# Converting fp64 weights: the mantissa's scale moved into VectorE's last product, the sign moved onto the power of two

## The chip, the cores and the metric

The kernel runs on one core of a Trainium2 chip. The metric is the device time of one execution in microseconds, lower is better. One program on one core is measured; three runs of the kernel before took 819.85, 822.35 and 826.33 us (median 822.35).

## What is computed

Two blocks follow each other. The first is a recurrence over 768 time steps for 4 batches x 8 heads with a 40 x 40 state; the second is a two-matrix feed-forward block over the 3072 tokens which the first produces, with `h * cos(h)` between the matrices.

```python
# recurrence, per batch and head: state is 40 x 40
y[:, :, t] = einsum('bhd,bhde->bhe', r_t, state)
Sa = einsum('bhde,bhe->bhd', state, a_t)
state = state * w_t[:, :, None, :] - outer(Sa, b_t) + outer(v_t, k_t)
# feed-forward: x is y as (3072, 320)
h = x @ w_in                 # 320 x 2048
g = h * np.cos(h)
out = (g @ w_out).astype(np.float32)   # 2048 x 320
```

The inputs of the recurrence are float32. The weights `w_in` and `w_out` reach the kernel as float64, because their scaling by `1/np.sqrt(...)` widens them. The chip's engines have no float64 arithmetic in this kernel, so each weight is put together from the two 32-bit words of its float64. `w_in` is also multiplied by 1/(2 pi), so that `h` comes out in turns, and `w_out` by 2 pi, which takes that back.

## The kernel before

**Two interleaved streams.** The recurrence is computed in 24 chunks of 32 time steps. Each chunk `c` has a chain of five segments, `t`, `q`, `x`, `s`, `z` (functions `ch_t` to `ch_z`): TensorE makes products in PSUM, ScalarE and VectorE copy or mask them to SBUF, the next segment's matmuls read those. The last segment, `ch_z`, updates the state `qz`: VectorE adds (line 656), GpSimd multiplies by the decay (line 657, four instructions), then GpSimd multiplies the outputs `yt` (line 668). The next chunk starts by transposing `qz` on TensorE (`ch_t`, line 558) and copying the result on ScalarE (`s`, line 562). The feed-forward block is cut into pieces (`first_a`, `first_b`, `second`) that are placed between the segments (`M` in the lists of segments), and fills TensorE for most of the run.

**The order is written out by hand.** The loop at line 920 lists the segments of each chunk; `step(work, of_inv, of_w)` runs one segment, then whatever was put off until then, then up to `of_w` steps from the list `w_steps`. Each engine takes its instructions in this order, so an instruction that waits holds up everything behind it on its engine.

**The weights' conversion** is 20 items of 128 x 512 numbers. Function `rounded` returns four closures for an item: `fetch` (SyncE issues the DMAs of the raw words), `taken`, `mantissa` and `product`. In what follows T(n), STT(n) and P(n) are VectorE's instructions of item n in those three:

- T(n), lines 241 and 242: from the high word, the 20 mantissa bits, and the 11 exponent bits. ScalarE then makes the power of two from the exponent (`expo`, line 245) and the sign as +1 or -1 (`sign`, line 247).
- STT(n), line 251: adds the low word times 2^-32 to the mantissa bits. ScalarE then makes `1 + m/2^20`, already times the factor, in one pass (`mant`, line 254, called ident(n) below).
- P(n), line 257: mantissa times power, written to the weights' tile. GpSimd then multiplies that tile by the sign in place (line 260).

The list `w_steps` (lines 840 to 849) puts them in the order P(n), fetch, STT(n+1), T(n+2), P(n+1) and so on; so T(n) stands two groups ahead of P(n). The tiles `mant`, `expo` and `sign` have two buffers each. GpSimd has other work in the same queue: the copies `vp`, `rp` (line 490), which wait for the DMAs of `v` and `r`, and `kn`, `vvm` (lines 497, 498). SyncE issues all loads of the recurrence and the weights in one queue.

**TensorE's fillers.** `busy` (line 856) puts matmuls on an unused tile between the first segments, whose results nobody reads.

Of the kernel before, what the change touches and what calls it, by code (L numbers as in the profile page):

```python
# [9 lines left out]
F32 = mybir.dt.float32  # L10
I32 = mybir.dt.int32
U32 = mybir.dt.uint32
ALU = mybir.AluOpType
ACTF = mybir.ActivationFunctionType
# [6 lines left out]
def kernel(  # L21
# [43 lines left out]
    nc = tc.nc  # L65
    B, H, S, D = r.shape
    P, C, DP = 128, 32, 64
# [22 lines left out]
    def kept(name, shape, n=1, fill=None, part=lambda t: t, on=nc.gpsimd):  # L90

        tiles = []
        for i in range(n):
            t = const.tile(shape, F32, tag=f"{name}{i}", name=f"{name}{i}")
            if fill is not None:
                on.memset(part(t), fill)
            tiles.append(t)
        return tiles
# [8 lines left out]
    src = {"r": r, "k": k, "v": v, "w": w, "a": a, "b": b}  # L107
# [12 lines left out]
    for n, fill in (("w", 1.0), ("a", 0.0), ("b", 0.0)):  # L120
        for i in range(4):
            x = slice((i - 2) * H * DP, (i - 1) * H * DP)
            if i < 2:
                t = const.tile([P, H, DP], F32, tag=f"nat_{n}{i}", name=f"nat_{n}{i}")
            else:
                t = {
                    "w": w_in_sb[:, 0, late:], "a": w_in_sb[:, 1, late:], "b": late_out
                }[n][:, x].rearrange("p (h d) -> p h d", h=H)
# [4 lines left out]
    for n in "kvr":  # L133
        t = const.tile([P, H, D], F32, tag=f"nat_{n}", name=f"nat_{n}")
# [69 lines left out]
    bn_b = kept("bn", [P, H, DP], 7, 0.0, padding)  # L204
    kn_b = kept("kn", [P, H, DP], 2, 0.0, padding)

    by_in = kept("by_in", [P, 1], 1, 0.5 / math.pi)[0]
    by_out = kept("by_out", [P, 1], 1, 2.0 * math.pi)[0]
    to_bits = kept("to_bits", [P, 1], 1, (127.0 - 1023) * 2**23)[0]


# [5 lines left out]
    WID = 512  # L217
    first_done, second_done = [], []

    def rounded(m, dst, src, by, by_sb):  # L220

        pool, tag = (
            ((sb2, "gT"), (sb2, "gT"), (sb1, "nt"), (sb1, "u"), (sb1, "inv"))[m % 5]
            if m < 10 else ((sb1, "nt"), (sb1, "u"), (sb1, "inv"))[(m - 10) % 3]
        )
        t = {}

        def fetch():  # L230
            t["words"] = pool.tile([P, WID, 2], I32, tag=tag, name="words")
            for rows, cols, part in src:
                nc.sync.dma_start(
                    t["words"][rows, cols].rearrange("p n w -> p (n w)"), part.bitcast(I32)
                )

        def taken():
            hi = t["words"][:, :, 1]
            t["mant"] = sb2.tile([P, WID], I32, tag="mant", name="mant")
            t["expo"] = sb2.tile([P, WID], I32, tag="expo", name="expo")  # L240
            nc.vector.tensor_scalar(t["mant"], hi, 0xFFFFF, None, ALU.bitwise_and)
            nc.vector.tensor_scalar(
                t["expo"], hi, 20, 0x7FF, ALU.logical_shift_right, ALU.bitwise_and
            )
            nc.scalar.activation(t["expo"], t["expo"], ACTF.Relu, bias=to_bits, scale=2.0**23)
            t["sign"] = sb2.tile([P, WID], mybir.dt.bfloat16, tag="sign", name="sign")
            nc.scalar.activation(t["sign"], hi, ACTF.Sign)

        def mantissa():
            frac = t["mant"].bitcast(F32)  # L250
            nc.vector.scalar_tensor_tensor(
                frac, t["words"][:, :, 0].bitcast(U32), 2.0**-32, t["mant"], ALU.mult, ALU.add
            )
            nc.scalar.activation(frac, frac, ACTF.Identity, bias=by_sb, scale=2.0**-20 * by)

        def product():
            nc.vector.tensor_tensor(
                dst, t["mant"].bitcast(F32), t["expo"].bitcast(F32), ALU.mult
            )
            nc.gpsimd.tensor_tensor(dst, dst, t["sign"], ALU.mult)  # L260

        return fetch, taken, mantissa, product

    def weights():


        wide = moe_w_in.dtype != F32
        work = []

        def put(dst, src, by, by_sb):  # L270
            if wide:
                work.append(rounded(len(work), dst, src, by, by_sb))
                return

            def fetch():
                for rows, cols, part in src:
                    nc.sync.dma_start(dst[rows, cols], part)

            none = lambda: None
            work.append((fetch, none, none, lambda: nc.scalar.mul(dst, dst, by)))  # L280

        flat_out = w_out_sb.rearrange("p f n -> p (f n)")
        for j in range(NF // 4):
            cs = slice(j * WID, (j + 1) * WID)
            for i in range(2):
                put(
                    w_in_sb[:, i, cs], [(every, slice(0, WID), moe_w_in[i * P : (i + 1) * P, cs])],
                    0.5 / math.pi, by_in,
                )
            if j % 2 == 0:  # L290
                put(
                    w_in_tail[:, j : j + 2].rearrange("p j f n -> p (j f n)"),
                    [
                        (
                            full[e], slice(2 * i * P, 2 * (i + 1) * P),
                            moe_w_in[2 * P :, (4 * (j + i) + 2 * e) * P : (4 * (j + i) + 2 * e + 2) * P],
                        )
                        for i in range(2)
                        for e in range(2)
                    ],  # L300
                    0.5 / math.pi, by_in,
                )
            first_done.append(len(work))
            for o in range(0, NF * DM, WID):
                if not 4 * j * DM <= o < 4 * (j + 1) * DM:
                    continue
                parts = []
                for f in range(o // DM, (o + WID - 1) // DM + 1):
                    lo, hi = max(o, f * DM), min(o + WID, (f + 1) * DM)
                    parts.append(  # L310
                        (
                            every, slice(lo - o, hi - o),
                            moe_w_out[f * P : (f + 1) * P, lo - f * DM : hi - f * DM],
                        )
                    )
                put(flat_out[:, o : o + WID], parts, 2.0 * math.pi, by_out)
            second_done.append(len(work))
        return work

# [503 lines left out]
    def main(c):  # L823
        def last():
            ch_z(c)
            if c + 2 < NCH:
                later(8 if c == 2 else 1, lambda: p2_kn(c + 2))

        return [lambda: ch_t(c), lambda: ch_q(c), lambda: ch_x(c), lambda: ch_s(c), last]

    with tc.manual_schedule():

        w_work = weights()
        w_count = [0]

# [84 lines left out]
        for c in range(NCH):  # L920
            t, q, x, s, z = main(c)
# [109 lines left out]
```

## Time and profile before

| What | Value |
|---|---|
| median of three runs | 822.35 us (819.85 to 826.33) |
| span of the profiled execution, first to last instruction | 823.7 us |
| TensorE busy | 746.9 us, 91% |
| VectorE busy | 509.3 us, 62% |
| ScalarE busy | 383.8 us, 47% |
| GpSimd busy | 201.3 us, 24% |
| the conversion, first T(0) to the end of the last line-260 product | 65.5 to 151.0 us |

The profile has one execution. Its span is 1.35 us above the median of the three runs, well inside their spread of 6.5 us. "Busy" is the time in which an engine had at least one compute instruction in hand. A group of instructions is shown by line, engine, output and input, with count, total and mean duration; "idle before" is the time its engine stood still ahead of it, with what ended the wait. Where two instructions of an engine overlap, the second is already in the pipeline or already taken up and waiting while the first ends.

### The profile page before, as it was taken

Reading aid. Unit: us, or ns where it says so; the run is one execution under the profiler, and the core shown is the slowest. Engines: PE = TensorE matmul, PEld = TensorE weight load, DVE = VectorE, ACT = ScalarE, POOL = GpSimd, SP = SyncE. Lnnn points to the kernel's source line nnn. Section 1 sums busy time; section 2 is a strip of 40 time slices with the busy share of each in tenths; the row PEclk is TensorE's granted clock in tenths of the full one; section 3 lists DMA queues with packets and bytes.
Section 4 is the critical chain, followed back from the end, with each engine's and each line's share of the span. In section 5 each row is a group of like instructions: output and inputs, shape, how many; then the busy total and the mean of one; then the engine's idle time right before and its main releaser. Section 6 shows DMA issues by size and latency. Waiting matters only on the chain.

```text
span 823.7 us, 37673 instructions
## 1 busy us (share of the span) xinstructions
PE 746.9 (91%) x16832; PEld 571.3 (69%) x16832; DVE 509.3 (62%) x1081; ACT 383.8 (47%) x707; POOL 201.3 (24%) x352
## 2 busy tenths in 40 slices
PE   3656778899689999999999999999999999999997
PEld 2534456677467777778777777777787777777775
DVE  6987887859645599354797553895444874332231
ACT  1214676544244553545446446435635445363352
POOL 5315554430214023212221230330330222201000
PEclk9757799899789999999999999999999999999999
DMA  8456663244043322333223323214310212101000
GB/s 120 78 132 168 173 162 104 46 119 69 25 98 84 64 59 52 69 100 65 54 37 71 68 63 67 61 37 65 66 41 24 45 35 52 21 21 37 20 17 16
DMA packets 183297, 55.66 MB, mean 68 GB/s; under 512 B 157152, under 2 KB 178656, under 8 KB 183136
## 3 DMA queue, kind: packets, MB, share of 16 engines
q1 hardware_dynamic: 180560, 51.95, 29.2%
q8 instruction: 132, 2.16, 1.1%
q10 hardware_dynamic: 2320, 0.98, 0.6%
q0 software_dynamic: 256, 0.33, 0.2%
q14 instruction: 29, 0.24, 0.1%
HBM read 42.07 MB, written 11.14 MB: 65 GB/s over the span
## 4 chain that ended last, share of the span: by engine, by line
PE 63%; DVE 19%; ACT 6%; DMA 4%; issue 3%; SPq 3%; POOL 1%; DVEq 0%; ACTq 0%; POOLq 0%
PE ph L101 22%; PE po L101 20%; DVE inv_tmp L468 4%; DVE inv L472 4%; PE x0ps L101 3%; PE dps L101 3%; SPq L152 3%; PE gram L101 2%; DVE rw L391 2%; PE vT L326 2%; PE sps L101 2%; PE qps L101 1%; DVE turns L732 1%; PE nps L101 1%; PE sT L558 1%
## 5 line engine op out<-in xcount | busy, mean ns | idle before, releaser
L101 PE MATMUL po<-w_out_sb,gT 128*128 128x320 f32 x768 | 227.0, 445 | 0.0
L101 PE MATMUL ph<-xT,w_in_sb 128*128 128x256 f32 x768 | 189.5, 393 | 4.8 <-DVE gT L740 3.8
L101 PEld LDWEIGHTS po<-w_out_sb,gT 128*128 128x128 f32 x768 | 142.4, 193 | 55.9 <-issue 4.2
L101 PEld LDWEIGHTS ph<-xT,w_in_sb 128*128 128x128 f32 x768 | 142.3, 194 | 33.9 <-issue 13.9
L730 ACT ACTIVATE turns<-ph,rnd 128x512 f32<-128x512 f32 x96 | 63.8, 685 | 157.2 <-PE ph L101 156.7
L732 DVE SCALAR_TENSOR_TENSOR turns<-turns,ph 128x512 f32<-128x512 f32 x96 | 63.8, 684 | 109.2 <-ACT turns L730 108.9
L740 DVE TENSOR_TENSOR gT<-ph,turns 128x512 f32<-128x512 f32 x96 | 65.6, 685 | 36.3 <-ACT turns L737 36.3
L657 POOL TENSOR_TENSOR qz<-qz,wc 128x160 f32<-128x160 f32 x92 | 43.2, 489 | 163.1 <-DVE qz L656 162.6
L472 DVE TENSOR_TENSOR inv<-inv,inv_tmp 128x31 f32<-128x31 f32 (+15 forms) x186 | 72.0, 387 | 6.4
L468 DVE TENSOR_TENSOR inv_tmp<-u,inv 128x31 f32<-128x31 f32 (+15 forms) x186 | 70.0, 376 | 4.4
L736 ACT ACTIVATE turns<-turns 128x512 f32<-128x512 f32 x96 | 60.2, 627 | 23.3 <-DVE turns L732 23.3
L737 ACT ACTIVATE turns<-turns,half_pi 128x512 f32<-128x512 f32 x96 | 69.3, 722 | 3.1
L490 POOL COPY vp<-nat_v 128x320 f32<-128x320 f32 x25 | 12.5, 501 | 182.9 <-DMA nat_v<-in_v_dram 144.1
L101 PE MATMUL ph<-xT,w_in_tail 64*128 64x256 f32 x384 | 54.8, 404 | 0.0
L656 DVE TENSOR_TENSOR qz<-dps,qz 128x160 f32<-128x160 f32 x92 | 28.9, 315 | 33.9 <-PE dps L101 33.8
L391 DVE RECIPROCAL rw<-nat_w 128x320 f32<-128x320 f32 x20 | 42.8, 2142 | 0.1
L562 ACT COPY s<-sT 128x512 f32<-128x512 f32 x46 | 24.5, 584 | 37.6 <-PE sT L558 37.6
L101 PEld LDWEIGHTS ph<-xT,w_in_tail 64*128 64x128 f32 x384 | 33.3, 187 | 10.4 <-issue 6.6
L668 POOL TENSOR_TENSOR yt<-yt,wb 128x512 f32<-128x512 f32 x24 | 31.3, 1306 | 22.4 <-DVE yt L663 22.4
L546 ACT COPY vvm<-gram 128x256 f32<-128x256 f32 x24 | 8.8, 368 | 55.6 <-DVE ag L541 55.3
L101 PEld LDWEIGHTS sps<-x,rt 32*32 32x32 f32 x1536 | 18.1, 109 | 21.6 <-issue 16.5
L101 PE MATMUL sps<-x,rt 32*32 32x72 f32 x1536 | 23.0, 240 | 10.7 <-DVE rt L476 9.0
(118 smaller groups left out, 1070.1 us busy)
## 6 DMA issues: line engine op xcount, KB each, us to landing
words<-in_moe_w_in_dram SPq DMA_DIRECT2D x8, 512.0 KB
nat_k<-in_k_dram SPq DMA_DIRECT2D x96, 40.0 KB
nat_v<-in_v_dram SPq DMA_DIRECT2D x96, 40.0 KB
nat_r<-in_r_dram SPq DMA_DIRECT2D x96, 40.0 KB
xd<-yt SPq DMA_DIRECT2D x48, 80.0 KB
out_dram<-ot SPq DMA_DIRECT2D x24, 160.0 KB
nat_b<-in_b_dram SPq DMA_DIRECT2D x88, 40.0 KB
wd<-ws SPq DMA_DIRECT2D x5, 640.0 KB
```

The costliest lines, as they stand in the source:

```text
L101: nc.tensor.matmul(o, lhsT=lhsT, rhs=rhs, start=start, stop=stop, skip_group_check=True)
L391: nc.vector.reciprocal(rw, wn)
L468: nc.vector.tensor_tensor(tmp, u[:, j : j + 1, :j].to_broadcast([P, C - j, j]), x[:, j:, j : j + 1].to_broadcast([P, C - j, j]), ALU.mult,)
L472: nc.vector.tensor_tensor(x[:, j:, :j], x[:, j:, :j], tmp, ALU.subtract)
L656: nc.vector.tensor_tensor(z, pick(dp, 0, (2 * N72 + C, 2), (N72, 2), (1, D)), z, ALU.add)
L657: nc.gpsimd.tensor_tensor(z, z, wc.rearrange("p (f m b) -> p f m b", f=2, m=2)[:, :, :, bb] .unsqueeze(3).to_broadcast([P, 2, 2, D]), ALU. ...
L668: nc.gpsimd.tensor_tensor(yt.rearrange("p j b t -> p (j b) t"), yt.rearrange("p j b t -> p (j b) t"), wx, ALU.mult)
L730: nc.scalar.activation(n, u, ACTF.Identity, bias=rnd, scale=1.0)
L732: nc.vector.scalar_tensor_tensor(n, n, -ROUND, u, ALU.add, ALU.subtract)
L736: nc.scalar.activation(n, n, ACTF.Abs)
L737: nc.scalar.activation(n, n, ACTF.Sin, bias=half_pi, scale=-2.0 * math.pi)
L740: nc.vector.tensor_tensor(gT[:, 2 * e : 2 * e + 2].rearrange("p f t -> p (f t)"), us[e], ns[e], ALU.mult)
```

## The change

The pass of ScalarE over the mantissa (line 254) is dropped. Its `1 +` becomes a bit: T(n) also ORs 0x100000 into the mantissa, so that the integer is 2^20 + m. Its factor becomes an immediate of P(n), which is now a `scalar_tensor_tensor` (mantissa times constant, times power). The sign is no longer multiplied into the finished weight after P(n); GpSimd multiplies it into the power of two, in `taken`, right behind ScalarE's sign, so that P(n) writes the finished weight. The two constants' tiles and their memsets go away, and with them a parameter of `rounded` and `put`.

```diff
-    by_in = kept("by_in", [P, 1], 1, 0.5 / math.pi)[0]
-    by_out = kept("by_out", [P, 1], 1, 2.0 * math.pi)[0]
...
-    def rounded(m, dst, src, by, by_sb):
+    def rounded(m, dst, src, by):
...
-            nc.vector.tensor_scalar(t["mant"], hi, 0xFFFFF, None, ALU.bitwise_and)
+            nc.vector.tensor_scalar(
+                t["mant"], hi, 0xFFFFF, 0x100000, ALU.bitwise_and, ALU.bitwise_or
+            )
...
             t["sign"] = sb2.tile([P, WID], mybir.dt.bfloat16, tag="sign", name="sign")
             nc.scalar.activation(t["sign"], hi, ACTF.Sign)
+            power = t["expo"].bitcast(F32)
+            nc.gpsimd.tensor_tensor(power, power, t["sign"], ALU.mult)
 
         def mantissa():
...
-            nc.scalar.activation(frac, frac, ACTF.Identity, bias=by_sb, scale=2.0**-20 * by)
 
         def product():
-            nc.vector.tensor_tensor(
-                dst, t["mant"].bitcast(F32), t["expo"].bitcast(F32), ALU.mult
-            )
-            nc.gpsimd.tensor_tensor(dst, dst, t["sign"], ALU.mult)
+            nc.vector.scalar_tensor_tensor(
+                dst, t["mant"].bitcast(F32), 2.0**-20 * by, t["expo"].bitcast(F32), ALU.mult, ALU.mult
+            )
```

The counts per item go from 4 VectorE, 3 ScalarE and 1 GpSimd instructions to 4, 2 and 1. The order of VectorE's and SyncE's instructions is the same in both kernels. In ScalarE's queue the 20 passes of line 254 are missing, and the rest keeps its order. In GpSimd's queue the product with the sign of item n stands where T(n) is emitted, before it stood where P(n) is emitted.

More of the change, by code (lines that the diff above doesn't have):

```diff
@@ L268, in weights, with put @@
         work = []
-        def put(dst, src, by, by_sb):
+        def put(dst, src, by):
             if wide:
-                work.append(rounded(len(work), dst, src, by, by_sb))
+                work.append(rounded(len(work), dst, src, by))
                 return
@@ L287, in weights @@
                     w_in_sb[:, i, cs], [(every, slice(0, WID), moe_w_in[i * P : (i + 1) * P, cs])],
-                    0.5 / math.pi, by_in,
+                    0.5 / math.pi,
                 )
@@ L300, in weights @@
                     ],
-                    0.5 / math.pi, by_in,
+                    0.5 / math.pi,
                 )
@@ L315, in weights @@
                     )
-                put(flat_out[:, o : o + WID], parts, 2.0 * math.pi, by_out)
+                put(flat_out[:, o : o + WID], parts, 2.0 * math.pi)
             second_done.append(len(work))
```

## The prediction

> **What bounds the kernel now.** I read the table by stretches first, because 91% TensorE over the whole span hides that the conversion's stretch differs from the rest. Columns: stretch and length, then busy time and count for TensorE's matmuls and weight loads, VectorE, ScalarE and GpSimd, then TensorE's granted clock, DMA share, GB/s.
>
> ```profile
> 65.00:155.00 90.00, 69.42 (x1582) 47.41 (x1580) 74.19 (x130) 60.89 (x105) 48.81 (x53) 0.84 0.51 139
> 400.00:600.00 200.00, 197.83 (x4732) 154.86 (x4727) 131.97 (x285) 99.86 (x187) 46.84 (x87) 1.00 0.29 58
> ```
>
> From 400 to 600 us TensorE is busy 99% at full clock: nothing that the change touches runs there, and any shift of the conversion's end is handed on to the end of the run unchanged. From 65 to 155 us TensorE is busy 77%, of which 18.8 us are fillers, at clock 0.84; VectorE has 82%, ScalarE 68%, GpSimd 54%. No engine is full: this stretch is bound by a chain that hops between them. All 20 items lie in it.
>
> Next I asked for the removed line alone, then for the chain of waits in this stretch.
>
> ```profile
> L254 ACT ACTIVATE mant<-mant,by_in x10: 718/722/734, 68.7 to 140.9; 128x512 f32<-128x512 f32 x10
> ...
>   DVE mant L251: 9.6, 8
> ...
>   DVE w_in_sb L257: 2.1, 2
>   DVE w_in_tail L257: 1.5, 2
>   DVE w_out_sb L257: 1.2, 2
> ```
>
> The pass takes 0.72 us, 20 times (14.46 us of ScalarE). Ahead of it ScalarE stands still 9.6 us for STT(n); because of it VectorE stands still only 2.1 + 1.5 + 1.2 = 4.8 us. ScalarE has slack, so its 14.46 us are not the saving. In the chain from 60 to 155 us line 254 has 6.6% of 95 us, 6.3 us: that is what can leave the chain.
>
> **What the Trainium skill says.** (1) "SBUF — State Buffer", section "Who interferes with whom": VectorE and GpSimd share a port pair under an exclusive lock; a VectorE instruction with two SBUF inputs or in a two-port mode blocks against a GpSimd instruction that reads SBUF, whoever is first wins, and one with at most one SBUF input outside those modes does not contend. The trace agrees: the first two lines here are VectorE, the third GpSimd (start, duration, what).
>
> ```profile
> 84.19 1.38 DVE L241 TENSOR_SCALAR mant<-words 128x512 int32<-128x512 int32 x1
> 85.48 0.42 DVE L242 TENSOR_SCALAR expo<-words 128x512 int32<-128x512 int32 x1
> ...
> 83.74 1.54 POOL L260 TENSOR_TENSOR w_out_sb<-w_out_sb,sign 128x512 f32<-128x512 f32 x1 [0.96 <-DVE w_out_sb L257]
> ```
>
> Line 241 takes 1.38 us instead of 0.42 us alone and ends 0.29 us after the GpSimd product at 85.28. So an item costs the pair: VectorE start to start 0.33 + 0.33 + 0.61 + 0.60 = 1.87 us, plus GpSimd 1.16 us uncontended, 3.03 us, which the change leaves as it is. (2) "VectorE: DVE Perf Modes", section on the perf-mode tier table: float32 `tensor_tensor` has only its 1x rate, so P(n) has no faster mode to lose. It gives no row for `scalar_tensor_tensor`; the trace does: 0.684 us at line 732 against 0.682 us at line 257. (3) "GPSIMD Engine Reference", section 3.1: about 2.6 cycles an element for two inputs, an estimate of 512 x 2.6 / 1.2 GHz = 1.11 us; the trace has 1.154 us at least. The moved product has the same shape and types, so 1.16 us alone, 1.3 to 1.5 beside VectorE.
>
> **The change, part by part.** Free: the OR in line 241 (line 242 already has two operations and takes 0.42 us like line 241), the `scalar_tensor_tensor` in P(n) (row above), two memsets of one column less, SyncE's queue and VectorE's order, which are the same in both kernels. What moves is who waits for whom. Before: STT(n), ident(n), P(n), then GpSimd, for whom nobody waits in the trace (TensorE's first use comes later). After: T(n), power, sign, GpSimd, P(n). VectorE now waits for GpSimd, and GpSimd's queue has loads in it.
>
> *A. Opening, a loss.* From the chain of waits, then VectorE's timeline:
>
> ```profile
> 69.03 2.51 DMA nat_r<-in_r_dram
> ...
> 71.69 0.45 POOL rp L490
> 72.14 1.55 POOL w_in_sb L260
> 73.69 2.94 POOL qz L657 x4
> ```
>
> ```profile
> 66.81 0.68 DVE L251 SCALAR_TENSOR_TENSOR mant<-words,mant 128x512 f32<-128x512 uint32 x1
> 69.44 0.69 DVE L257 TENSOR_TENSOR w_in_sb<-mant,expo 128x512 f32<-128x512 f32 x1 [1.95 <-ACT mant L254]
> 70.05 0.32 DVE L656 TENSOR_TENSOR qz<-dps,qz 128x160 f32<-128x160 f32 x1
> ```
>
> GpSimd stands behind the DMA of `r` until 72.14. After the change both first sign products queue there, ahead of the state's products: 72.14 to 73.3 and 73.3 to 74.5. P(0), ready at 69.44 before, needs the first and finds the lock with the second: about 74.5. Queued behind P(0) on VectorE are the eight instructions of lines 656 and 663 (1.8 us), then STT(1). So line 656 starts near 75.1 instead of 70.05, and the first line 657 near 75.5 instead of 73.66. But those four then run beside instructions with one SBUF input, at the 1.89 us that four took at 102.1 us, instead of 2.97 us: end 77.3 against 76.63. TensorE's transposes wait for that. Loss **0.7 us on the chain**; STT(1) slips by 5.1 us (76.9 against 71.77), and the items follow late. I bound the loss by 0.5 and 3 us and take 1.0.
>
> *B. Items 2 to 9, 76 to 105 us, near nothing.* Before, items follow each other at 3.3 us (P(2) 79.14, P(3) 82.98, P(4) 86.27, P(5) 89.12). After: from the end of T(n), ScalarE 0.65 + 0.66 and a hand-over, GpSimd ready at 1.5 us; VectorE meanwhile does P(n-1), STT(n), line 241 (1.54 us); GpSimd takes the lock, 1.16; line 242 0.35: P(n) at 3.1. As long as before. ScalarE's copies of the recurrence stand behind `sign(n)`, hence behind T(n), so they inherit what is left of A's lag, 0 to 2.5 us; with the six waits of 4.8 us gone and DMA less bunched I take 0.5.
>
> *C. Where ident(n) stood last ahead of the recurrence, a gain.*
>
> ```profile
> 117.40 0.61 DVE mant L251
> ...
> 118.09 0.72 ACT mant L254
> 118.81 0.58 ACT turns L730
> ```
>
> Here `turns` waits for STT(13) and the pass: 1.2 us at most, and VectorE's line 732 behind it. The same before the `sm` copies at 98.25 (0.63), `s` at 141.53 (0.6), `wb` at 144.42 (0.6): 3.0 us. TensorE is continuously busy from 124.1 to 141.2 us and swallows part. Between 0 and 5 us; I take 2.0.
>
> *D. State update at 135 us, a loss.* The sign product of one item further stands ahead of line 657: its sign ends at 135.1, the product at 136.3, against a start of line 657 at 135.64. Loss 0.7 (0 to 1).
>
> *E. Last item, a loss.* T(19) ends at 147.05; 0.7 + 0.65 + 0.1 + 1.2 gives P(19) near 149.8 against 149.10: 0.7 (0 to 1). Behind it on VectorE stand line 397 and the reciprocal of line 391, which the next loads wait for.
>
> Sum: 1.0 + 0.5 - 2.0 + 0.7 + 0.7 = **+0.9 us**, 824.6 against the profiled span of 823.7, which stands 1.35 above the median of 822.35: **823.3 us**.
>
> **Rivals.** *Slower: VectorE held by GpSimd.* The path of an item after T(n) is 3.1 us against VectorE's own 1.87 us; if the lock and late queue-mates (`kn`, `vp` behind a DMA, `bn`) expose the difference of 1.2 us in 10 to 20 items, that is 12 to 24 us, less the 4.8 us of ended waits: 7 to 19 us, some 830 to 841. For it: A shows this in full once. Against: VectorE is already lock-bound where it is dense. It decides for over 1% from (8.2 + 4.8) / 20 = 0.65 us exposed per item. *Faster: the 6.3 us leave the chain whole*, with some of the 9.6 us of ScalarE's waiting, and A hides behind the DMA: 811 to 817. Against: the copies wait for `sign(n)` too, which remains. *No effect*: TensorE's fillers and the DMAs of the words (chain pieces of 2.52 and 2.10 us at 107.0 and 112.8) set the pace: 822. That the pass does not vanish is excluded: the changed program has none of the 20 in ScalarE's queue.
>
> Unknown besides: TensorE's clock, 0.5 to 0.6 for about 4 us after each long gap in this stretch (124 to 128 us: 0.57). One gap more or less is worth 1.8 us either way (the eight `ph` matmuls at 124.1 took 3.65 us, against 1.89 at 112.7).
>
> **How the numbers follow.** The sum and no effect together 0.65, 818 to 828; slower rival 0.23, of which 0.18 lies over 1%; faster rival 0.12, of which 0.08 over 1%. About 1% (8.2 us) is what a measurement of this kernel tells from no change. So faster 0.08, within 1% 0.74, slower 0.18. The range takes the sum's bounds and the near part of both rivals: 815 to 832.
>
> **What would show it.** A: the idle time of P(0) named GpSimd and about 5 us longer, line 657 first near 75.5. B: items at about 3.1 us, VectorE's idle for GpSimd below 0.3 us an item after the first. C: `turns` right after `x` near 117 to 119. ScalarE's busy time down by 14.4 us to about 369. Wrong would be waits of VectorE for GpSimd of over 10 us in sum, or conversion ends more than 3 us from 151.0.

## The result and the profile after

The changed kernel takes 826.18 us (median of 15 runs, 824.5 to 830.01) against 823.1 us for the kernel before (15 runs, 819.85 to 830.99). The ratio is 1.0042, 95% interval 1.0026 to 1.0058: 3.5 us slower by the ratio, within the 1% of the forecast, and clear of no change.

The spans of the two profiled executions say the opposite (822.8 after, 823.7 before). A second profile of the kernel before (below) has 819.6: it was 1.5 us ahead already at T(0) (64.01 us instead of 65.47), and its DMA of `r` let go of GpSimd at 68.8 us instead of 71.7. So single spans cannot rank these kernels. I therefore measure the **stage** inside each profile: from the start of T(0) (first instruction of line 241 or its successor) to the start of P(19). Before it is 149.10 - 65.47 = 83.6 us (83.0 in the second profile), after 151.95 - 65.93 = 86.0 us: +2.4 to +3.0 us, in step with the ratio. The two ends, before and then after (start, duration, what, and in brackets the idle time ahead with what ended it):

```profile
65.47 0.42 DVE L241 TENSOR_SCALAR mant<-words 128x512 int32<-128x512 int32 x1
...
149.10 0.71 DVE L257 TENSOR_TENSOR w_out_sb<-mant,expo 128x512 f32<-128x512 f32 x1 [0.85 <-ACT mant L254]
```

```profile
65.93 0.42 DVE L239 TENSOR_SCALAR mant<-words 128x512 int32<-128x512 int32 x1
...
151.95 0.69 DVE L258 SCALAR_TENSOR_TENSOR w_out_sb<-mant,expo 128x512 f32<-128x512 f32 x1 [1.46 <-POOL expo L249]
```

The two stretches of the kernel after, columns as in the prediction:

```profile
65.00:155.00 90.00, 70.19 (x1582) 46.90 (x1581) 71.14 (x128) 47.09 (x84) 43.30 (x50) 0.85 0.50 137
400.00:600.00 200.00, 197.92 (x4667) 154.74 (x4668) 131.80 (x284) 100.17 (x187) 46.40 (x86) 1.00 0.28 58
```

ScalarE lost 13.8 us in the first stretch (60.89 to 47.09), and no more work was done in it: VectorE has 128 instructions there, before 130. The second stretch is unchanged. The moved product, queried by its line (line 249 now): whom it waited for and, below the dots, who waited for it (us, times).

```profile
  ACT sign L247: 23.5, 13
...
  DVE w_in_sb L258: 4.3, 1
  DVE w_out_sb L258: 2.6, 2
  DVE w_in_tail L258: 2.1, 2
```

VectorE had waited 4.8 us for line 254; it now waits five times for GpSimd's product, for which nobody waited before, 8.9 us in sum (before rounding). The first wait, in the chain of waits of the kernel after (start, duration, what):

```profile
70.61 0.46 POOL rp L490
71.07 1.12 POOL expo L249
72.19 0.02 issue
72.22 0.08 DVE w_in_sb L258
...
72.39 1.37 issue
73.76 0.32 DVE qz L656
74.08 0.07 issue
74.15 1.75 POOL qz L657 x4
```

The copy that waits for `r`, the first sign product, then P(0), then the state's line 656. The 1.37 us of "issue" lie inside P(0), which was taken up at 72.22 while GpSimd had the second sign product in hand until 73.29. The timeline shows the two sign products (GpSimd, first line), one long P(0), 1.62 us instead of 0.68, and what stood behind it on VectorE:

```profile
71.03 2.26 POOL L249 TENSOR_TENSOR expo<-expo,sign 128x512 f32<-128x512 f32 x2
...
72.22 1.62 DVE L258 SCALAR_TENSOR_TENSOR w_in_sb<-mant,expo 128x512 f32<-128x512 f32 x1 [4.26 <-POOL expo L249]
73.76 0.31 DVE L656 TENSOR_TENSOR qz<-dps,qz 128x160 f32<-128x160 f32 x1
...
75.48 0.97 DVE L253 SCALAR_TENSOR_TENSOR mant<-words,mant 128x512 f32<-128x512 uint32 x1
```

ScalarE's timeline shows where the lag enters the recurrence:

```profile
78.28 0.72 ACT L245 ACTIVATE expo<-expo,to_bits 128x512 int32<-128x512 int32 x1 [9.03 <-DVE expo L242]
78.91 0.66 ACT L247 ACTIVATE sign<-words 128x512 bf16<-128x512 int32 x1
79.48 1.06 ACT L562 COPY s<-sT 128x512 f32<-128x512 f32 x2
```

The transposed state (`sT`) was finished at 76.8 us, but the copy `s` stands behind `expo(2)` and `sign(2)`, which wait for T(2), which VectorE does after the late STT(1). In the kernel before, `s` waited only for TensorE and started at 77.41 us, though there `r` had come 1.08 us later:

```profile
77.41 1.07 ACT L562 COPY s<-sT 128x512 f32<-128x512 f32 x2 [1.46 <-PE sT L558]
```

### The profile page after: what moved, and what is told of

It is laid out like the page before. It is cut to its first block, busy times and chain, and to the rows that moved or that the text cites. A ratio compares the mean times of both kernels' runs of the same rounds, so it can differ in the third digit from the quotient of the medians.

```text
span 822.8 us, 37659 instructions
## 1 busy us (share of the span) xinstructions
PE 744.5 (90%) x16832; PEld 569.3 (69%) x16832; DVE 508.8 (62%) x1081; ACT 370.8 (45%) x687; POOL 197.9 (24%) x350
## 4 chain that ended last, share of the span: by engine, by line
PE 64%; DVE 20%; ACT 5%; issue 4%; DMA 3%; SPq 2%; POOL 2%; DVEq 0%; ACTq 0%; POOLq 0%
PE ph L101 22%; PE po L101 20%; DVE inv_tmp L468 4%; DVE inv L472 4%; PE x0ps L101 3%; PE dps L101 3%; DVE rw L391 3%; PE gram L101 3%; PE vT L326 2%; PE sps L101 2%; PE nps L101 2%; SPq L152 2%; PE qps L101 1%; DVE turns L732 1%; PE sT L558 1%
## 5 line engine op out<-in xcount | busy, mean ns | idle before, releaser
L101 PE MATMUL ph<-xT,w_in_sb 128*128 128x256 f32 x768 | 187.0, 389 | 4.6 <-DVE gT L740 3.7
L546 ACT COPY vvm<-gram 128x256 f32<-128x256 f32 x24 | 8.9, 369 | 57.5 <-DVE ag L541 57.1
```

What stands on the lines that cost most here:

```text
L101: nc.tensor.matmul(o, lhsT=lhsT, rhs=rhs, start=start, stop=stop, skip_group_check=True)
```

## The experiments

Theory 1: the missing pass is a small gain, and the sign's new place is the loss, because VectorE's P(n) now waits for GpSimd, whose queue stands behind the DMA of `r` in the opening. Theory 2: the opening makes the whole loss. Theory 3: the missing pass itself hurts, by shifting other work against each other. Each ratio is to the kernel before, timed again beside the others; e2 rests on 6 runs, e6 on 7, the others on 14 to 22. Stage is as defined above, in one profile each; the two profiles of the kernel before differ by 0.6 us in it, e1 and e7, one kernel, by 1.1 us.

| Kernel | ratio to before | 95% interval | stage, us |
|---|---|---|---|
| before, first and second profile | 1.0015 (control) | 0.9998 to 1.0033 | 83.6, 83.0 |
| full change | 1.0042 | 1.0026 to 1.0058 | 86.0 |
| e1 pass gone, sign last | 0.9983 | 0.9967 to 0.9999 | 81.2 |
| e7 the same again | 0.9981 | 0.9966 to 0.9997 | 80.1 |
| e2 pass kept, sign early | 1.0085 | 1.0056 to 1.0114 | 90.0 |
| e3 full, items 0 and 1 signed last | 1.0007 | 0.9992 to 1.0022 | 84.3 |
| e4 only items 0 and 1 early | 1.0002 | 0.9983 to 1.0021 | 83.7 |
| e5 sign by bits on VectorE | 0.9964 | 0.9946 to 0.9982 | 80.5 |
| e6 sign left out | 0.9928 | 0.9903 to 0.9953 | 77.7 |
| e8 full, copies put off | 0.9998 | 0.9980 to 1.0015 | 84.4 |
| e9 before, copies put off | 1.0011 | 0.9996 to 1.0025 | 83.2 |
| e10 bits, copies put off | 0.9958 | 0.9944 to 0.9972 | 82.4 |
| e11 sign last, copies put off | 0.9954 | 0.9937 to 0.9972 | 80.5 |

**Control.** No edit.

> The kernel before, unchanged, as a measure of what two measurements of the same kernel differ by, and for a second profile of it. All theories expect a ratio of 1.000 with an interval of about 0.0015 to 0.002 on each side. In the trace, the last P(19) should start within 1.5 us of 149.1 us once the landing of the DMA of r (71.5 us in the first profile) is taken off, and VectorE should wait about 5 us in sum for ScalarE's line 254.

The two measurements of one kernel differ by 0.0015: differences of 0.002 between two rows are at the edge of what is resolved. P(19) started 2.1 us earlier than in the first profile, at 147.00, and 1.5 us of these were there at T(0) already.

**The two halves of the change.** e1 against the full change:

```diff
-            power = t["expo"].bitcast(F32)
-            nc.gpsimd.tensor_tensor(power, power, t["sign"], ALU.mult)
...
         def product():
...
+            nc.gpsimd.tensor_tensor(dst, dst, t["sign"], ALU.mult)
```

> One half of the change alone: ScalarE's pass is gone and the factor is in P(n), but GpSimd multiplies the finished weight by the sign after P(n), as before. Theory 1 (the loss comes from VectorE waiting for GpSimd, the pass alone is a gain where it stood ahead of the recurrence's copies): ratio 0.995 to 0.999, P(0) near 68 us, P(19) 1 to 3 us earlier than before. Theory 2 (the loss is made in the opening alone, by the first two items): the same sign, 0.994 to 0.998. Theory 3 (it is the missing pass that hurts, by shifting other transfers or copies against each other, not the sign's place): 1.002 to 1.006.

e2 against the kernel before:

```diff
             nc.scalar.activation(t["sign"], hi, ACTF.Sign)
+            power = t["expo"].bitcast(F32)
+            nc.gpsimd.tensor_tensor(power, power, t["sign"], ALU.mult)
...
-            nc.gpsimd.tensor_tensor(dst, dst, t["sign"], ALU.mult)
```

> The other half alone: ScalarE's pass stays, the sign is multiplied into the power right behind ScalarE's sign. Theory 1: slower than the full change, since the wait for GpSimd is there and the pass too: ratio 1.005 to 1.009, VectorE waiting for GpSimd about 9 us in sum. Theory 2: about 1.006, with the loss in place by 80 us and not growing. Theory 3: 0.999 to 1.001.

Theory 3 falls: the pass gone alone is faster, 0.9983 and 0.9981 in two measurements (-1.5 us), and the sign early alone is slower by 7.0 us. With the pass gone, the sign's move costs 1.0042 - 0.9982 = 0.0060, 4.9 us. The pass is worth more when the sign is early (1.0085 to 1.0042, 3.5 us) than when it is last (1.5 us), but with e2's wide interval this difference of 0.0025 is not clear of noise. TensorE's clock does not explain the 4.9 us: its mean over all runs is 0.9521 with the full change and 0.9534 and 0.9537 in e1 and e7, and by a straight line through the runs of each of these kernels 0.01 of clock goes with 2 to 3 us, an estimate of under 0.6 us for the difference. The waits of VectorE in e2 (line 259 there is P(n), line 256 the pass; us in total, times, longest):

```profile
DVE w_in_sb L259 <- POOL expo L249: 6.5, 1, 6.5
...
DVE w_in_tail L259 <- POOL expo L249: 1.6, 1, 1.6
...
DVE w_out_sb L259 <- ACT mant L256: 1.4, 1, 1.4
```

P(n) has two providers there, and waits now for the one, now for the other.

**How much the opening makes.** e3 and e4 are complements; e3 against the full change, e4 with the conditions exchanged:

```diff
+            if m >= 2:
                 power = t["expo"].bitcast(F32)
                 nc.gpsimd.tensor_tensor(power, power, t["sign"], ALU.mult)
...
         def product():
...
+            if m < 2:
+                nc.gpsimd.tensor_tensor(dst, dst, t["sign"], ALU.mult)
```

> The full change, but for items 0 and 1 GpSimd multiplies the finished weight by the sign after P(n), so that nothing on VectorE waits behind the DMA of r in GpSimd's queue. Theory 1: the opening's part goes (VectorE's wait of 4.3 us for GpSimd at item 0), the later waits at items 2, 4, 12 and 19 stay (about 4.6 us in sum): ratio 1.000 to 1.003. Theory 2: the gain of the missing pass shows whole, 0.994 to 0.999. Theory 3: no change against the full change, 1.003 to 1.006.

> The complement of the run in which items 0 and 1 alone were signed last: here items 0 and 1 alone have the sign in the power, all others are signed after P(n); ScalarE's pass is gone throughout. Theory 1a (most of the loss is made where P(0) waits in VectorE's queue for GpSimd, which waits for the DMA of r; about 2.9 us of the 4.9 us between sign last and sign early): ratio 1.001 to 1.003. Theory 1b (the loss is spread over the 20 items, and the opening only brings the lag forward): 0.998 to 1.000.

e3 takes back 0.0035 (2.9 us) of the 0.0060. e4 loses 0.0020 (1.7 us) against e1 and e7; its interval touches both theories, so its time alone decides nothing, but its stage is 2.5 to 3.6 us longer than theirs. Its P(0) shows why (VectorE, then GpSimd ahead of it):

```profile
73.65 1.62 DVE L259 SCALAR_TENSOR_TENSOR w_in_sb<-mant,expo 128x512 f32<-128x512 f32 x1 [6.17 <-POOL expo L250]
```

```profile
72.05 0.45 POOL L493 COPY rp<-nat_r 128x320 f32<-128x320 f32 x1 [3.31 <-DMA nat_r<-in_r_dram]
72.46 2.26 POOL L250 TENSOR_TENSOR expo<-expo,sign 128x512 f32<-128x512 f32 x2
```

So two of twenty items make roughly a third to three fifths of what the sign's move costs. The profiles agree: from T(0) to the copy `x` of chunk 1 the full change takes 26.2 us, e1 and e7 23.6 and 23.0; from there to P(19) it takes 59.8 us, they 57.6 and 57.1. About as much is lost behind the opening as in it, by one profile each. Theory 2 is too strong: e3 is still 0.0025 above e1 and e7, and still has waits of P(n) for GpSimd:

```profile
DVE w_in_tail L259 <- POOL expo L250: 4.2, 2, 3.1
...
DVE w_out_sb L259 <- POOL expo L250: 2.5, 2, 1.4
```

Which of these waits make the rest of the loss, no run took apart.

**What the product on GpSimd costs at all.** e5 against the full change: ScalarE's sign and GpSimd's product go away, and VectorE copies the sign bit.

```diff
-            t["sign"] = sb2.tile([P, WID], mybir.dt.bfloat16, tag="sign", name="sign")
-            nc.scalar.activation(t["sign"], hi, ACTF.Sign)
-            power = t["expo"].bitcast(F32)
-            nc.gpsimd.tensor_tensor(power, power, t["sign"], ALU.mult)
...
         def mantissa():
...
+            nc.vector.scalar_tensor_tensor(
+                t["expo"], t["words"][:, :, 1], -(2**31), t["expo"], ALU.bitwise_and, ALU.bitwise_or
+            )
```

> No GpSimd product and no sign on ScalarE: in the mantissa step VectorE takes the sign bit from the high word and ORs it into the power (one more scalar_tensor_tensor of 0.68 us an item, 0.60 start to start). Per item VectorE gains 0.60 us of own work (12 us in sum) and loses the lock held by GpSimd (1.16 us an item, 23 us in sum); ScalarE loses 13.3 us. Theory 1 (the path T(n), power, sign, GpSimd, P(n) and the lock bound the stretch): ratio 0.990 to 0.997. Rival (VectorE's own instructions bound the stretch, it is busy 82% there): 1.003 to 1.010.

e6 drops only the two lines of GpSimd's product, so its weights lack their sign.

> The full change without GpSimd's 20 products, so the weights lack their sign; ScalarE still computes it. It bounds what the sign's place and the lock can cost together. Theory 1: below the run with the sign last by what the lock costs VectorE: 0.991 to 0.997. If only P(n)'s wait counts and the lock is hidden: as the sign last, 0.997 to 1.000.

Both fell where theory 1 put them. Adding 12 us of VectorE work in place of 23 us of GpSimd work (and 13 us of ScalarE's sign) made the stage shorter, so VectorE's own instructions are not all that bounds it. They are not free either: e5, with 20 more of them than e6 and without ScalarE's sign, is slower by 0.0036, 3.0 us, just clear of noise. Even with the sign last, where P(n) does not wait for it, the product costs 0.9982 - 0.9928 = 0.0054, 4.4 us. Part of that can be waits of others, who in e1 (line 259 is the product there) were ScalarE's sign and the state's addition:

```profile
  ACT sign L247: 2.6, 3
  DVE qz L655: 1.0, 1
```

The stretch of e6:

```profile
65.00:155.00 90.00, 74.16 (x1673) 50.13 (x1671) 71.04 (x145) 51.12 (x91) 22.63 (x37) 0.87 0.54 143
```

VectorE finishes 145 instructions in 71.0 us there, against 128 in 71.1 us with the full change. The counts mix sizes, but the same holds for like instructions: the 40 of T(n), lines 239 and 242, sum to 28.1 us in e1, 28.2 in e7 and 20.0 in e6. So part of VectorE's "busy" time had been waiting inside instructions. That agrees with the Trainium skill's "SBUF — State Buffer", section "Who interferes with whom", as the prediction used it. What the lock alone costs the run was not isolated: e6 takes the product's work and place away too.

**Is it the DMA in GpSimd's queue?** In e8 to e11 the copies `vp`, `rp` of chunk 2 come one step later, behind the state's products:

```diff
-                later(1, lambda: p2_in(c + 1))
+                later(2 if c == 1 else 1, lambda: p2_in(c + 1))
```

> The full change, and GpSimd's copies vp and rp of chunk 2, which wait for the DMA of r, stand one step later in its queue: behind the first two sign products, the state's products and yt. Theory 1 (in the opening P(0) waits because GpSimd's queue stands behind that DMA): VectorE's first wait for GpSimd shrinks from 4.3 us to about 2 us or less, and the ratio falls by 0.003 to 0.006 against the full change's 1.0042: 0.998 to 1.001. If the DMA is not what the loss hangs on (the lock and the two products themselves): 1.002 to 1.004.

> The kernel before with the same two copies put off, as the control: what they cost without the change. The chain of waits of the kernel before runs from the DMA of r through the copy, the sign product of item 0 and the state's products into TensorE, so some of it may go here too: ratio 0.995 to 0.999. Theory 1 expects the full change to lose less against this control than it loses against the kernel before, 0.001 to 0.003 instead of 0.0042; if the DMA is not the point, the distance stays at 0.004.

The full change falls from 1.0042 to 0.9998, no slower than its control e9 (1.0011). GpSimd and VectorE in e8:

```profile
68.99 2.33 POOL L249 TENSOR_TENSOR expo<-expo,sign 128x512 f32<-128x512 f32 x2 [24.52 <-ACT sign L247]
72.19 1.75 POOL L657 TENSOR_TENSOR qz<-qz,wc 128x160 f32<-128x160 f32 x4 [0.86 <-DVE qz L656]
...
75.55 0.65 POOL L490 COPY vp<-nat_v 128x320 f32<-128x320 f32 x1
```

```profile
70.18 1.69 DVE L258 SCALAR_TENSOR_TENSOR w_in_sb<-mant,expo 128x512 f32<-128x512 f32 x1 [1.40 <-POOL expo L249]
```

The sign products start when ScalarE's sign is there, and P(0) waits 1.40 us instead of 4.26: its long wait did hang on the DMA ahead of it in GpSimd's queue. Behind the opening the waits stay: 5.0 us in sum in e8, and from `x` to P(19) it takes 60.6 us, e9 59.1. The expectation for the control was a miss: putting the copies off did not make the kernel before faster (1.0011 instead of 0.995 to 0.999). Its state's products started 1.8 us earlier than in the first profile of before, but by the copy `x` of chunk 1 only 0.4 us was left (90.08 against 90.52; T(0) itself was 0.5 us later). Why, no run took apart.

> Sign by bits on VectorE, the pass gone, and the copies put off: a candidate for beating both kernels. If the two gains add: 0.991 to 0.995. If the sign by bits had already taken what the copies hold up: 0.996 as without.

> Pass gone, sign last, copies put off. If the gains add: 0.993 to 0.997; if the opening is only bound by other loads (k, v, r of the next chunk are issued in the same queue): 0.998 as without.

e11 (0.9954) and e10 (0.9958) are the fastest here of those with the sign, and beat both kernels, by 3.5 to 3.8 us against before. For e10 the bits had already taken it (0.9964 without). e11 gained 0.0028 on e1 and e7. Between e5, e10 and e11 the intervals overlap.

e11 also limits what e8 shows. Putting the copies off gave 0.0044 with the sign early and 0.0028 with the sign last, so what it took from the sign's move as such is 0.0016, 1.3 us, which is not clear of noise. With the copies put off, the early sign still costs 0.9998 - 0.9954 = 0.0044, 3.6 us. The DMA in the queue makes P(0)'s wait, but the sign's move is dear without it too.

## Why the prediction was right, and which terms were mis-sized

The forecast was 823.3 us with no change within 1% likeliest, and the range held the time. That alone says little: 1% is 8.2 us, and it is not the limit of the measurement, as the prediction had it, since the intervals here are 0.14 to 0.29% wide on each side. The mechanism was right: a small gain from the pass, and larger losses from VectorE waiting for GpSimd. The sum of +0.9 us was too low; measured is +3.5 us. The gain was 1.5 us where 2.0 stood, the losses 4.9 where 2.9 stood.

- *What bounds the kernel:* right in the main. Shifts of the stage reach the end: from e6 (77.7 us, 0.9928) to e2 (90.0 us, 1.0085) stages and ratios grow together, but not one for one within 2 us of stage; e10's stage is 1.9 us longer than e5's and e8's 1.2 us longer than e9's, while their ratios are not higher.
- *A, the opening:* the times were close. Line 656 was put 3.4 us behind the start of `rp` and was found 3.15 us behind (73.76 - 70.61); STT(1) was to slip by 5.1 us and slipped by 4.8 (4.87 us behind `rp` against 0.08). The last state's product ended 5.29 us behind `rp` against 4.94, a loss of 0.35 where 0.7 stood.
- *B, the step that failed by its size:* "ScalarE's copies of the recurrence ... inherit what is left of A's lag, 0 to 2.5 us; ... I take 0.5". The copy `s` of chunk 1 started 8.87 us behind `rp` against 5.72, 3.15 us late, beyond the bound, and `x` at 92.16 against 90.52. e3 prices the opening at 2.9 us, e4 at 1.7 us, A and the lag of B together had 1.5. What is left of the 4.9 us, 2.0 to 3.2 us, is lost behind the opening, where D and E had 1.4. The items' period was right: P(3), P(4), P(5) of the kernel after stand 3.05 and 2.88 us apart, predicted 3.1.

```profile
84.86 0.68 DVE L258 SCALAR_TENSOR_TENSOR w_out_sb<-mant,expo 128x512 f32<-128x512 f32 x1
...
87.91 0.69 DVE L258 SCALAR_TENSOR_TENSOR w_out_sb<-mant,expo 128x512 f32<-128x512 f32 x1 [1.09 <-POOL expo L249]
...
90.79 0.68 DVE L258 SCALAR_TENSOR_TENSOR w_out_sb<-mant,expo 128x512 f32<-128x512 f32 x1
```

- *C, the gain:* 2.0 us taken; the pass alone measured 1.5 us (e1, e7), so the faster rival's 6.3 us did not leave the chain whole. At the place shown, nothing was gained (before, then after):

```profile
116.52 0.39 ACT L599 COPY x<-x0ps 128x288 f32<-128x288 f32 x1
...
120.14 0.63 ACT L736 ACTIVATE turns<-turns 128x512 f32<-128x512 f32 x1 [0.17 <-DVE turns L732]
```

```profile
118.06 0.40 ACT L599 COPY x<-x0ps 128x288 f32<-128x288 f32 x1 [0.96 <-PE x0ps L101]
119.09 0.69 ACT L730 ACTIVATE turns<-ph,rnd 128x512 f32<-128x512 f32 x1 [0.63 <-PE ph L101]
121.02 0.69 ACT L730 ACTIVATE turns<-ph,rnd 128x512 f32<-128x512 f32 x1 [1.24 <-PE ph L101]
121.61 0.62 ACT L736 ACTIVATE turns<-turns 128x512 f32<-128x512 f32 x1
```

From `x` to the first line 736 it is 3.55 us, and was 3.62 before: the second `turns` now waits 1.24 us for TensorE's `ph`, a wait that had run beside the pass.

- *D and E:* as said. The third state update starts at 138.12, after a sign product from 137.00, 2.5 us later than before, some 1.8 of them lag. P(19) waits 1.46 us for GpSimd, where it had waited 0.85 for ScalarE: 0.6, predicted 0.7.
- *Signs named:* VectorE's waits for GpSimd after the first were 4.6 us over 19 items, 0.24 each (below 0.3), 8.9 in sum (below 10). The conversion ended at 152.6 us, 1.6 us from 151.0 (below 3). ScalarE fell to 370.8 us, not 369: the 14.46 us of the passes include what overlapped with a neighbour, which is one likely reason.

The slower rival's place was right, its price was not: VectorE's waits for GpSimd came at five items, not at 10 to 20.

## What to carry to other kernels

When a step moves from behind the last product to ahead of it, ask what else stands in that engine's queue: here a helper for whom nobody waited became a provider, behind a copy that waits for a DMA. A lag of one engine is not over when its consumer has caught up; follow it through each in-order queue it passes (VectorE to ScalarE's copies to TensorE). A pass that is removed gives only what the chain waited for: 1.5 us here of 14.5 us of busy time. And test a repair on the other variants too: putting off the copies helped the kernel with the sign last too (0.0028, against 0.0044 with the sign early).

## What was not expected of the hardware

Two profiles of one kernel differ by 4.1 us of span (823.7 and 819.6): 1.5 us of it stood at T(0), 2.9 us at the copy behind the DMA of `r` (71.7 and 68.8 us), 2.1 us at P(19). And 12 us more of VectorE instructions in place of GpSimd's 23 us and ScalarE's 13 us shortened the stage by about 5.5 us (86.0 to 80.5).
